# A mean over features made by two float32r products instead of one float32 product

## The chip, the core and the metric

The kernel runs on one core of one Trainium2 chip. A core has a matrix engine (TensorE, PE in the profile), a vector engine (VectorE, DVE), a scalar engine (ScalarE, ACT), a general engine (GpSimd, POOL) and DMA queues, most of them fed here by the sync engine (SyncE, SP). The metric is the device time of one execution in microseconds. The kernel before takes 1026.13 us in the median of three runs (1026.02 to 1029.73).

## The reference, cut to what matters

Three layers follow each other on inputs of 4 batches, 768 positions and 512 features: a chunked attention with 8 heads, a Fourier mixer with a dense block, and a gated convolution block. The change lies in the Fourier mixer, between the transform and the normalization:

```python
X = np.fft.fft(x, axis=1)
X = np.fft.fft(X, axis=2)
u = x + np.real(X)
mu = np.mean(u, axis=-1, keepdims=True)
un = (u - mu) / np.sqrt(np.mean((u - mu) ** 2, axis=-1, keepdims=True) + 1e-06)
ch = np.maximum(un @ w_ch1, 0.0) @ w_ch2
x = u + ch
```

## The kernel before, in words

The program is one long hand-written order. A string of letters (`SCHED`) names the next piece of work for the first two parts: S, E, A, P and X are attention steps of one block of 96 positions (scores, exponentials, transposes, product with the values, transposes of the result), W is a step of decoding a weight, F is a filler product on PE (`keep`), B is the next step of the Fourier transform of a batch (`dft`, a generator that gives up the turn at each `yield`) and D is the next step of the first part of the dense block (`dense`). Each engine executes what it is given in the order in which the program was written, so a letter that adds an instruction to an engine puts it ahead of everything that later letters give to that engine. The first two parts last to about 335 us; the rest of the dense block and the convolution block follow.

Features lie on the 128 partitions, positions along the free dimension. `dft(b)` folds the input (`F`, split in a high float32r part and the rest, `Fh` and `Fl` in the tile `Fhl`), multiplies it with a table (`zstep`, PSUM tile `z`, split again to `zh` by ACT and `zl` by DVE), multiplies that with a second table (PSUM tile `p`) and adds to the spectrum, tiles `G` and `H`, one of even and one of odd parts. The mean over the 512 features needs `G` alone: the two feature blocks of `G` are added (`summed`, tile `gs`, on POOL, one half of 384 positions at a time), and a product with a matrix of constants (`onesm`) sums over the partitions and writes the sum to all partitions (`center`, PSUM tile `pm`). DVE then takes `pm` off `G`, ACT copies one row of `pm` back to the first row of `gs`, and SP writes this row to DRAM (`mud`), from where a later stage reads the mean.

The order around it, for each batch: `summed(0)`, two `zstep`s (c = 2), `center(0)`, `summed(1)`, two `zstep`s (c = 3), `center(1)`. So `summed(1)` is written directly behind `center(0)`, and since `gs` is one buffer, POOL's sum of the second half waits until the row of the first half has been written to DRAM. There are 4 batches and 8 such products.

The names in the rows: `sm` are the attention scores, `atp` and `xtp` PSUM tiles of transposes, `at` and `xT` their copies, `o` the product with the values, `h`, `hh`, `hl`, `y` the tiles of the dense block, `wsc`, `wlb`, `whb` the steps of decoding a weight. `atp`, `xtp`, `idle`, `z`, `p`, `pm`, `h` and `y` take turns in four PSUM buffers (`ps_g`, `PSG = 4`); a new one waits until the copies out of the old one are done. All products of the helper `accumulate` show line 65, the product of `center` line 415.

Of the kernel before, what the change touches and what calls it, by code (L numbers as in the profile page):

```python
# [7 lines left out]
F32 = mybir.dt.float32  # L8
F32R = mybir.dt.float32r
AF = mybir.ActivationFunctionType  # L10
ALU = mybir.AluOpType
# [15 lines left out]
HALF = S // 2  # L27
# [18 lines left out]
def fourier_mixer_kernel(ctx: ExitStack, tc: tile.TileContext, qk, vw, w1, w2, w_in, w_out, conv_w,  # L46
                         mask, ident, dtab, orow, stab, sgn, out):
    nc = tc.nc
    mm = nc.tensor.matmul
# [12 lines left out]
    def accumulate(o, seq, start=True, stop=True):  # L62
        n = len(seq)
        for i, (a, b) in enumerate(seq):
            mm(o, a, b, start=(start and i == 0), stop=(stop and i == n - 1))  # L65

    const = ctx.enter_context(tc.tile_pool(name="const", bufs=1))
    epsc = const.tile([128, 1], F32, name="epsc")
    nc.vector.memset(epsc, 1e-6)
    onesm = const.tile([128, 128], F32, name="onesm")  # L70
    nc.vector.memset(onesm, 2.0 / DM)
    expb = const.tile([128, 1], F32, name="expb")
    nc.vector.memset(expb, -float(EXP0 << 23))
    expl = const.tile([128, 1], F32, name="expl")
# [227 lines left out]
    def dft(b):  # L302
# [10 lines left out]
        Fhl = dfp.tile([128, 20, 193], F32R, tag="Fhl", name="Fhl")  # L313
# [13 lines left out]
        def zstep(c, m):  # L327
            w = SIZES[c]
            w0 = (w + 1) // 2
            s0, sn = (0, w0) if m == 0 else (w0, w - w0)  # L330
            cols = slice(0, CW) if c < 2 else slice(CW, CW + SW)
            nw = CW if c < 2 else SW
            z = ps_g.tile([128, 512], F32, tag="g", name="z")
            terms = []
            for kt in range(2):
                f = FOFF[c] + kt
                terms.append((Fh[:, f, s0:s0 + sn], Fl[:, f, s0:s0 + sn],
                              dtab_sb[:, 0, kt, cols], dtab_sb[:, 1, kt, cols]))
            seq = split3(terms)
            if c < 2:  # L340
                f = FOFF[c] + 2
                seq += [(Fh[0:1, f, s0:s0 + sn], orow_sb), (Fl[0:1, f, s0:s0 + sn], orow_sb)]
            accumulate(z[:sn, 0:nw], seq)
            zh = dfp.tile([97, 256], F32R, tag=f"zh{c % 2}{m}", name="zh")
            zl = dfp.tile([97, 256], F32R, tag=f"zl{c % 2}{m}", name="zl")
            nc.scalar.copy(zh[:sn], z[:sn, 0:256])
            if c < 2:
                zn = dfp.tile([97, 2, 2], F32R, tag=f"zn{c}{m}", name="zn")
                nc.scalar.copy(zn[:sn, 0], z[:sn, 256:258])
            nc.vector.tensor_tensor(out=zl[:sn], in0=z[:sn, 0:256], in1=zh[:sn].bitcast(F32), op=ALU.subtract)  # L350
            if c < 2:
                nc.vector.tensor_tensor(out=zn[:sn, 1], in0=z[:sn, 256:258], in1=zn[:sn, 0].bitcast(F32),
                                        op=ALU.subtract)
                ZN[c, m] = zn
            Z[c, m] = (zh, zl, sn)
# [34 lines left out]
        for m in range(2):  # L390
            zc = slice(128 * m, 128 * m + 128)
            p = ps_g.tile([128, 512], F32, tag="g", name="p")
# [4 lines left out]
                                    in0=pj[:, 0:192, :],  # L397
                                    in1=xT[:, m, 0:384].rearrange("p (j r) -> p j r", r=2), op=ALU.add)
            nc.vector.tensor_tensor(out=G[:, m, 384:385], in0=p[:, 192:193], in1=xT[:, m, 384:385], op=ALU.add)
            nc.vector.tensor_tensor(out=G[:, m, 385:769].rearrange("p (j r) -> p j r", r=2),  # L400
                                    in0=pj[:, 191::-1, ::-1],
                                    in1=xT[:, m, 385:769].rearrange("p (j r) -> p j r", r=2), op=ALU.add)
# [3 lines left out]
        def summed(hf):  # L406
            gs = dfp.tile([128, HALF], F32, tag="gs", name="gs")
            ss = slice(hf * HALF, hf * HALF + HALF)
            nc.gpsimd.tensor_tensor(out=gs, in0=G[:, 0, ss], in1=G[:, 1, ss], op=ALU.add)
            return gs  # L410

        def center(hf, gs):
            ss = slice(hf * HALF, hf * HALF + HALF)
            pm = ps_g.tile([128, 512], F32, tag="g", name="pm")
            mm(pm[:, 0:HALF], onesm, gs, start=True, stop=True)
            for m in range(2):
                nc.vector.tensor_tensor(out=G[:, m, ss], in0=G[:, m, ss], in1=pm[:, 0:HALF], op=ALU.subtract)
            nc.scalar.copy(gs[0:1, :], pm[0:1, 0:HALF])
            nc.sync.dma_start(out=mud[b][:, ss], in_=gs[0:1, :])

        gs = summed(0)
        for c in (2, 3):
            for m in range(2):
                zstep(c, m)
                yield
            center(c - 2, gs)
            if c == 2:
                gs = summed(1)
            yield
        for m in range(2):  # L430
            zc = slice(128 * m, 128 * m + 128)
            p = ps_g.tile([128, 512], F32, tag="g", name="p")
            for c, o, n in ((2, 0, 194), (3, 256, 192)):
                seq = part(c, n, zc)
                accumulate(p[:, o:o + n], seq[:-1], stop=False)
                if m == 0:
# [4 lines left out]
                                    in1=pj[:, 0:192, :],  # L441
                                    in0=xT[:, 2 + m, 0:384].rearrange("p (j r) -> p j r", r=2), op=ALU.subtract)
# [99 lines left out]
    def task(k):  # L542
# [5 lines left out]
        if k == "S":  # L548
            scores(n)
            load_qk(n + 2)  # L550
            if n == 0:
                load_v(2)
        elif k == "E":
            expo(n // 2, n % 2)
            if n == 8:
                nc.gpsimd.dma_start(out=dtab_sb, in_=dtab)
                nc.gpsimd.dma_start(out=orow_sb, in_=orow)
                nc.gpsimd.dma_start(out=stab_sb, in_=stab)
        elif k == "A":
            atr(n // 2, n % 2)  # L560
        elif k == "P":
            pv(n)
            load_v(n + 3)
        elif k == "X":
            xtr(n)
            if n % NU == NU - 2:
                bga.append(dft(n // NU))
        elif k == "F":
            keep(1)
        elif k == "B":  # L570
            return step_of(bga)
        elif k == "D":
            return step_of(bgb)
        else:
            return run(todo[k])
        return True

    with tc.manual_schedule():
# [43 lines left out]
        ps_g.release()  # L622
        ps_g = tc.alloc_tile_pool(name="ps_g2", bufs=3, space=PSUM, reuse_waits="tile")
        uc1 = tc.alloc_tile_pool(name="uc1", bufs=1, reuse_waits="tile")
        onesr = uc1.tile([128, 128], F32R, name="onesr")
        nc.vector.tensor_copy(onesr, onesm)
        NC1 = NB * S // TC

        FS = (range(NI, NI + NGA), range(NI + NGA, NF1), range(NI, NF1))
# [110 lines left out]
        for i, (s, f) in enumerate(seq):  # L740
            c, fs, last = steps[s]
# [283 lines left out]
```

## Time and profile before

| | |
|---|---|
| median of three runs | 1026.13 us (1026.02 to 1029.73) |
| span of the profiled execution, first to last instruction | 1023.3 us |
| PE busy | 1006.2 us, 98% |
| DVE busy | 681.6 us, 67% |
| ACT busy | 442.7 us, 43% |
| POOL busy | 216.8 us, 21% |
| granted clock of PE, mean | 1.000 |
| products `pm` | 8, in 16 records, from 94.2 to 301.6 us |

The span is that of one profiled execution, 2.8 us under the median of the timed runs, which hold the start and the end of the execution too. PE's busy time counts pipelined products whose ends are modelled, so that starts of successive products are the better measure of what one costs.

### The profile page before, as it was taken

How to read it: one execution, taken by the hardware profiler on the slowest of the kernel's cores; microseconds unless marked ns; L12 is line 12 of the kernel's file. 1: busy time of each engine (PE TensorE's matmuls, PEld its weight loads, DVE VectorE, ACT ScalarE, POOL GpSimd, SP SyncE). 2: the span in 40 equal slices, each digit the busy share in tenths (PEclk: the TensorE clock that was granted, in tenths of full speed). 3: DMA queues.
4: the chain of work that ended last, by engine and by line, in shares of the span. 5: the costliest groups of instructions: out<-in, count | busy, mean ns of one | idle time of the engine just before them, and what ended most of it. 6: DMA issues, size and time to landing. Idle time of an engine off the chain costs nothing.

```text
span 1023.3 us, 16696 instructions
## 1 busy us (share of the span) xinstructions
PE 1006.2 (98%) x6446; PEld 959.4 (94%) x6446; DVE 681.6 (67%) x1500; ACT 442.7 (43%) x923; POOL 216.8 (21%) x230
## 2 busy tenths in 40 slices
PE   7899999999999999999999999999999999999998
PEld 6888989999999999999999999999999999999996
DVE  4889956756888766767787775635358566465554
ACT  4687754665433433233333232312245454454442
POOL 1363251432500000112210100202013222222222
PEclk9999999999999999999999999999999999999999
DMA  6864532522236554675879872727543211010101
GB/s 201 265 191 135 170 109 74 159 76 80 104 104 211 185 172 165 204 172 129 196 199 219 200 188 89 112 85 131 180 115 113 70 62 62 1 62 1 62 1 62
DMA packets 63776, 130.87 MB, mean 128 GB/s; under 512 B 4887, under 2 KB 39167, under 8 KB 63471
## 3 DMA queue, kind: packets, MB, share of 16 engines
q1 hardware_dynamic: 51424, 102.35, 30.4%
q0 software_dynamic: 12016, 27.16, 14.7%
q8 instruction: 51, 0.84, 0.3%
q10 hardware_dynamic: 256, 0.28, 0.1%
q14 instruction: 29, 0.24, 0.1%
HBM read 92.28 MB, written 43.79 MB: 133 GB/s over the span
## 4 chain that ended last, share of the span: by engine, by line
PE 90%; DVE 5%; issue 2%; DMA 1%; ACT 1%; POOL 0%; DVEq 0%; ACTq 0%; POOLq 0%
PE acc L65 32%; PE h L65 24%; PE ph L65 12%; PE y L65 5%; PE o L266 4%; PE sc L232 3%; PE z L65 3%; PE p L65 2%; PE atp L255 2%; PE idle L206 1%; PE xtp L291 1%; DVE sm L238 1%; DMA yd<-y 1%; DVE uc L165 1%; DVE wlb L128 0%
## 5 line engine op out<-in xcount | busy, mean ns | idle before, releaser
L65 PE MATMUL acc<-hh,w 128*128 128x384 f32 x768 | 208.0, 334 | 0.0
L65 PE MATMUL h<-uh,w 128*128 128x384 f32 x768 | 208.0, 334 | 0.0
L485 ACT ACTIVATE hh<-h 128x384 fp32r<-128x384 f32 x128 | 62.4, 490 | 247.4 <-PE h L65 247.4
L486 DVE SCALAR_TENSOR_TENSOR hl<-h,hh 128x384 fp32r<-128x384 f32 x128 | 70.6, 555 | 148.2 <-ACT hh L485 147.9
L65 PEld LDWEIGHTS acc<-hh,w 128*128 128x128 f32 x768 | 139.8, 188 | 0.0
L65 PEld LDWEIGHTS h<-uh,w 128*128 128x128 f32 x768 | 139.8, 188 | 0.0
L65 PE MATMUL ph<-xh,wit 128*128 128x384 f32 x512 | 136.3, 337 | 0.7 <-ACT hrow L815 0.7
L65 PE MATMUL acc<-hl,w 128*128 128x384 f32 x384 | 128.3, 334 | 0.0
L65 PE MATMUL h<-ul,w 128*128 128x384 f32 x384 | 128.3, 334 | 0.0
L65 PE MATMUL acc<-wot,hgh 128*128 128x512 f32 x384 | 119.6, 393 | 0.0
L823 DVE SCALAR_TENSOR_TENSOR cv<-hrow,cw_sb,cv 128x768 f32<-128x768 f32 x64 | 110.1, 1721 | 3.1 <-ACT cv L817 2.0
L835 POOL TENSOR_TENSOR hgl<-cv,hgh 128x768 fp32r<-128x768 f32 x32 | 60.3, 1885 | 194.7 <-ACT hgh L834 179.0
L829 DVE TENSOR_TENSOR cv<-hrow,cv 128x768 f32<-128x768 f32 x32 | 30.7, 959 | 99.1 <-ACT cv L828 99.1
L65 PEld LDWEIGHTS ph<-xh,wit 128*128 128x128 f32 x512 | 93.3, 188 | 2.6 <-ACT hrow L815 1.4
L65 PE MATMUL ph<-xl,wit 128*128 128x384 f32 x256 | 86.1, 336 | 0.0
L65 PEld LDWEIGHTS acc<-wot,hgh 128*128 128x128 f32 x384 | 71.7, 188 | 13.4
L246 ACT ACTIVATE sm<-sm,ngm 96x128 f32<-96x128 f32 x256 | 80.5, 392 | 7.3 <-DVE ngm L238 7.3
L815 ACT ACTIVATE hrow<-ph 128x384 f32<-128x384 f32 x64 | 31.2, 493 | 102.3 <-PE ph L65 101.1
L65 PE MATMUL acc<-wot,hgl 128*128 128x512 f32 x192 | 74.7, 389 | 0.0
L65 PEld LDWEIGHTS acc<-hl,w 128*128 128x128 f32 x384 | 72.1, 188 | 0.0
L65 PEld LDWEIGHTS h<-ul,w 128*128 128x128 f32 x384 | 72.1, 188 | 0.0
L238 DVE CUSTOM_DVE_ANT_0 sm<-sc,mask_sb 96x128 f32<-96x128 f32 x256 | 56.3, 281 | 18.6 <-PE sc L232 14.6
(148 smaller groups left out, 1881.3 us busy)
## 6 DMA issues: line engine op xcount, KB each, us to landing
w<-in_w SPq DMA_DIRECT2D x32, 512.0 KB, 4.1
qk<-in_qk SPq DMA_DIRECT2D x32, 448.0 KB, 3.4
us<-ucd SPq DMA_DIRECT2D x13, 768.0 KB, 6.8
yp<-yd SPq DMA_DIRECT2D x13, 768.0 KB, 7.9
vw<-in_vw SPq DMA_DIRECT2D x32, 260.0 KB, 2.9
ucd<-uc SPq DMA_DIRECT2D x8, 768.0 KB, 4.5
yd<-y SPq DMA_DIRECT2D x32, 192.0 KB, 1.9
ucd<-mud POOLq DMA_DIRECT2D x8, 768.0 KB, 14.5
```

The source lines that it names most:

```text
L65: mm(o, a, b, start=(start and i == 0), stop=(stop and i == n - 1))
L232: mm(sch[2 * a + g], qT[64 * g:64 * g + 64, a, :], kT[64 * g:64 * g + 64, a, :], start=True, stop=True)
L238: nc.vector.tensor_tensor_reduce(out=sm[:, h, :], in0=sch[h], in1=mask_sb[:, kind, :], op0=ALU.add, op1=ALU.min, scale=-0.125, scalar=3e38 ...
L246: nc.scalar.activation(out=d["ex"][:, h, :], in_=d["ex"][:, h, :], func=AF.Exp, scale=-1.0, bias=d["ngm"][:, h:h + 1])
L255: nc.tensor.transpose(at[:, i, :], d["ex"][:, 4 * half + i, :], ident_sb[:QB, :QB])
L266: mm(oh[:, h // 4, h % 4, :], at_sb[:, h, :], vw[:, h * (HD + 1):(h + 1) * (HD + 1)], start=True, stop=True)
L485: nc.scalar.activation(out=hh, in_=p[:, 0:TC], func=AF.Relu)
L486: nc.vector.scalar_tensor_tensor(out=hl, in0=p[:, 0:TC], scalar=0.0, in1=hh.bitcast(F32), op0=ALU.max, op1=ALU.subtract)
L815: nc.scalar.activation(out=h[:, 1 + hf * TC:1 + hf * TC + TC], in_=p[:, 0:TC], func=AF.Relu)
L823: nc.vector.scalar_tensor_tensor(out=cv, in0=h[:, j:j + S], scalar=cw_sb[:, j, f:f + 1], in1=cv, op0=ALU.mult, op1=ALU.add)
L829: nc.vector.tensor_tensor(out=cv, in0=h[:, 1:S + 1], in1=cv, op=ALU.mult)
L835: nc.gpsimd.tensor_tensor(out=hgl[i], in0=cv, in1=hgh[i].bitcast(F32), op=ALU.subtract)
```

## The change

The constants get a float32r copy (`onesr`) that is now made at the start of the program, no longer in a later part. `summed` splits its sum: ACT copies `gs` to a float32r tile `gh`, DVE subtracts it from `gs` and writes the rest to `gl`. Both lie in parts of the tile `Fhl` that are no longer needed. `center` multiplies `gh` and `gl` with `onesr`, in two float32r products that add up in `pm`.

```diff
     nc.vector.memset(onesm, 2.0 / DM)
+    onesr = const.tile([128, 128], F32R, name="onesr")
+    nc.vector.tensor_copy(onesr, onesm)
...
             nc.gpsimd.tensor_tensor(out=gs, in0=G[:, 0, ss], in1=G[:, 1, ss], op=ALU.add)
-            return gs
-
-        def center(hf, gs):
+            gh, gl = (Fhl[:, k:k + 2].rearrange("p n w -> p (n w)")[:, 0:HALF] for k in (0, 3))
+            nc.scalar.copy(gh, gs)
+            nc.vector.tensor_tensor(out=gl, in0=gs, in1=gh.bitcast(F32), op=ALU.subtract)
+            return gs, gh, gl
+
+        def center(hf, gs, gh, gl):
             ss = slice(hf * HALF, hf * HALF + HALF)
             pm = ps_g.tile([128, 512], F32, tag="g", name="pm")
-            mm(pm[:, 0:HALF], onesm, gs, start=True, stop=True)
+            accumulate(pm[:, 0:HALF], [(onesr, gh), (onesr, gl)])
...
-            center(c - 2, gs)
+            center(c - 2, *gs)
...
-        onesr = uc1.tile([128, 128], F32R, name="onesr")
-        nc.vector.tensor_copy(onesr, onesm)
```

The order on ACT in the first batch, before; `gs<-pm` is the row of the mean, `zh` the split of the products `z`:

```order
L162 COPY at<-atp 128x384
L346 CAST zh<-z 96x256
L127 ACTIVATE wsc<-wsc,expl 128x512
L346 CAST zh<-z 96x256
L418 COPY gs<-pm 1x384
L346 CAST zh<-z 97x256
L346 CAST zh<-z 96x256
L296 ACTIVATE xT<-xtp 128x4x96
```

The same place on ACT now; `Fhl<-gs` is the new copy `gh`:

```order
L164 COPY at<-atp 128x384
L413 CAST Fhl<-gs 128x384
L348 CAST zh<-z 96x256
L129 ACTIVATE wsc<-wsc,expl 128x512
L348 CAST zh<-z 96x256
L423 COPY gs<-pm 1x384
L413 CAST Fhl<-gs 128x384
L348 CAST zh<-z 97x256
L348 CAST zh<-z 96x256
L298 ACTIVATE xT<-xtp 128x4x96
```

The first copy stands ahead of both `zh` of c = 2, the second directly behind the row of the mean and ahead of both `zh` of c = 3.

The order on ACT in the third batch, around the row of the first half, before:

```order
L162 COPY y<-y 128x384
L346 CAST zh<-z 96x256 x2
L162 COPY at<-atp 128x384
L418 COPY gs<-pm 1x384
L162 COPY at<-atp 128x384
L346 CAST zh<-z 97x256
```

The same place on ACT now:

```order
L164 COPY y<-y 128x384
L413 CAST Fhl<-gs 128x384
L348 CAST zh<-z 96x256 x2
L164 COPY at<-atp 128x384
L423 COPY gs<-pm 1x384
L413 CAST Fhl<-gs 128x384
L164 COPY at<-atp 128x384
L348 CAST zh<-z 97x256
```

Here the second copy stands ahead of a copy `at` out of a PSUM buffer.

The order on DVE in the fourth batch, at the second half of the mean, before:

```order
L417 TENSOR_TENSOR G<-G,pm 128x384 x2
L135 TENSOR_SCALAR wsc<-whb 128x512
L139 SCALAR_TENSOR_TENSOR w_5_3822<-wlb,wsc 128x512
L123 TENSOR_SCALAR wsc<-w_4113 128x512
L124 TENSOR_SCALAR wlb<-w_4113 128x512
L128 SCALAR_TENSOR_TENSOR wlb<-w_4113,wlb 128x512
L350 TENSOR_TENSOR zl<-z,zh 97x256
```

The same place on DVE now; `Fhl<-gs,Fhl` is the new subtraction `gl`:

```order
L422 TENSOR_TENSOR G<-G,pm 128x384 x2
L414 TENSOR_TENSOR Fhl<-gs,Fhl 128x384
L137 TENSOR_SCALAR wsc<-whb 128x512
L141 SCALAR_TENSOR_TENSOR w_5_3842<-wlb,wsc 128x512
L125 TENSOR_SCALAR wsc<-w_4133 128x512
L126 TENSOR_SCALAR wlb<-w_4133 128x512
L130 SCALAR_TENSOR_TENSOR wlb<-w_4133,wlb 128x512
L352 TENSOR_TENSOR zl<-z,zh 97x256
```

The subtraction stands behind the one that takes the mean off `G`, and ahead of five steps of decoding and the next `zl`.

## Rows read from the trace of the kernel before

**Rows 1.** The page: the span, and busy time, share and instructions of each engine

```profile
span 1023.3 us, 16696 instructions
PE 1006.2 (98%) x6446; PEld 959.4 (94%) x6446; DVE 681.6 (67%) x1500; ACT 442.7 (43%) x923; POOL 216.8 (21%) x230
```

**Rows 2.** Busy us by stretch: length, PE, PEld, DVE, ACT, POOL, clock, DMA share, GB/s

```profile
0.00:85.00 85.00, 76.02 (x757) 67.20 (x758) 62.91 (x342) 58.60 (x171) 30.54 (x54) 1.00 0.69 212
85.00:110.00 25.00, 24.83 (x250) 22.79 (x249) 22.53 (x93) 16.84 (x51) 6.67 (x12) 1.00 0.43 129
```

**Rows 3.** Waits of PE up to 335 us: the longest (total, times, longest)

```profile
PE sc L232 <- DMA qk<-in_qk: 2.2, 1, 2.2
```

**Rows 4.** Instructions on gs and pm: ns min/median/max, first and last start, form

```profile
L409 POOL TENSOR_TENSOR gs<-G x8: 864/866/871, 93.2 to 297.3; 128x384 f32<-128x384 f32 x8
L418 ACT COPY gs<-pm x8: 467/469/471, 96.7 to 305.5; 1x384 f32<-1x384 f32 x8
L417 DVE TENSOR_TENSOR G<-G,pm x16: 539/545/554, 95.6 to 304.9; 128x384 f32<-128x384 f32 x16
```

**Rows 5.** Timeline of PE, second batch: start, duration, instruction [idle before it, and releaser]

```profile
166.06 0.84 PE L415 MATMUL pm<-gs,onesm 128*128 128x384 f32 x2
...
166.91 0.33 PE L65 MATMUL h<-ul,rxa 128*128 128x384 f32 x1
167.07 0.34 PE L65 MATMUL h<-uh,rxb 128*128 128x384 f32 x1
```

**Rows 6.** Timeline of the first batch, several engines

```profile
93.24 0.87 POOL L409 TENSOR_TENSOR gs<-G 128x384 f32<-128x384 f32 x1 [1.85 <-DVE G L396]
...
93.71 0.42 DVE L350 TENSOR_TENSOR zl<-z,zh 96x256 fp32r<-96x256 f32 x1
...
95.58 1.01 DVE L417 TENSOR_TENSOR G<-G,pm 128x384 f32<-128x384 f32 x2
...
96.68 0.47 ACT L418 COPY gs<-pm 1x384 f32<-1x384 f32 x1 [2.12 <-DVE G L417]
97.06 0.62 ACT L346 CAST zh<-z 97x256 fp32r<-97x256 f32 x2
97.17 0.31 SPq L419 DMA_DIRECT2D mud<-gs  x1
...
98.42 0.86 POOL L409 TENSOR_TENSOR gs<-G 128x384 f32<-128x384 f32 x1 [4.32 <-ACT sm L246]
...
101.89 0.46 ACT L162 COPY at<-atp 128x384 f32<-128x384 f32 x1
...
103.10 0.45 PE L65 MATMUL p<-stab_sb,zh 96*128 96x194 f32 x2
```

**Rows 7.** Timeline of the second batch, ACT and PE

```profile
169.03 0.49 ACT L485 ACTIVATE hh<-h 128x384 fp32r<-128x384 f32 x1 [0.53 <-PE h L65]
...
172.81 0.33 PE L65 MATMUL y<-hh,rxc 128*128 128x384 f32 x1
```

**Rows 8.** Timeline of the third batch, ACT, SP and PE

```profile
233.95 0.46 ACT L162 COPY at<-atp 128x384 f32<-128x384 f32 x1
...
234.07 0.24 SPq L419 DMA_DIRECT2D mud<-gs  x1
...
234.47 0.44 PE L65 MATMUL y<-hh,rxc 128*128 128x384 f32 x1
```

**Rows 9.** Timeline of the fourth batch, DVE, SP and PE

```profile
295.39 0.42 DVE L135 TENSOR_SCALAR wsc<-whb 128x512 int32<-128x512 int32 x1
...
296.05 0.24 SPq L419 DMA_DIRECT2D mud<-gs  x1
...
297.36 1.34 DVE L128 SCALAR_TENSOR_TENSOR wlb<-w,wlb 128x512 int32<-128x512 int32 x1
298.62 0.41 DVE L350 TENSOR_TENSOR zl<-z,zh 97x256 fp32r<-97x256 f32 x1
...
299.09 0.45 PE L65 MATMUL h<-uh,rxa 128*128 128x384 f32 x1
```

## The prediction

> **What bounds the kernel now.** First the busy times of the page: PE is busy 1006 of 1023 us, so some 17 us of idle time are left in all [rows 1]. Then the busy times by stretch: 9 of these 17 us lie in the first 85 us; where the change works, PE has 0.2 us of idle time in 25 us, and DVE is nearly as full, 22.5 of 25 us [rows 2]. So the end is set by PE's list: what shortens it is gained, and what makes PE wait is lost, for hardly any idle time is left behind it to give the loss back. Then the timelines around the eight means. PE, ACT and DVE each take their lists in order, so the question for every added instruction is what it waits for and what stands behind it.
>
> **What is saved.** The float32 product starts at 166.06; the second `h` product behind it starts at 166.91, and such products follow each other by 0.16 us, so the first `h` began at about 166.74 and the mean cost 0.68 us [rows 5]. Two float32r products of the same 384 columns cost 2 x 0.16 to 0.17, or 0.33. Saved: 0.35 us at each of 8 places, 2.8 us, all on PE.
>
> **What is added.** Eight copies on ACT and eight subtractions on DVE. The nearest rows are ACT's copy of 384 columns, 0.47 us, and DVE's subtraction of as many, 0.55 us [rows 4]. If they merely filled idle time they would cost nothing; DVE has too little of it for that in the first batch, and the waits are worse than the work. The copy waits for POOL's sum `gs`, the subtraction for the copy, and both stand ahead of what PE wants next. The copy `onesr` moves from the later part to the start, where DVE has nothing else to do: nothing.
>
> The second half of each mean is the bad one. Its `gs` waits until the first half's row is in DRAM. In the first batch: ACT starts that row at 96.68, SP issues the transfer at 97.17, 0.49 later, and POOL starts at 98.42, 1.25 after the issue [rows 6]; POOL needs 0.87 [rows 4]. Until now nobody but PE waited for that, much later. Now ACT stops behind the row's copy until 0.49 + 1.25 + 0.87 = 2.6 us after its start, which is some 2.2 us of standing still, then copies 0.47, and DVE, which had finished with `G` before the row was copied, stands still for 3.1 us before its 0.55. Everything that the two have behind that comes later. What PE feels of it differs from batch to batch.
>
> First batch. POOL's first sum ends at 94.11 (93.24 + 0.87), the copy at about 94.64, the subtraction at about 95.2. DVE used to start `zl` at 93.71 and `G` minus `pm` at 95.58 [rows 6]; it now starts that list at 95.2, 1.5 us later, and the row of the mean starts at 98.1. By the sum above, POOL's second sum starts at 99.85 and ends at 100.72, and the copy ends at 101.25. ACT's `zh`, formerly at 97.06, starts at about 101.2, a shift of 4.1 us. From there ACT is busy almost without a break to the copy `at` at 101.89 (to 102.35), and the second half of PE's products `o` waits for this copy: eight heads, then `p` at 103.10 [rows 6]. So `p` comes at 107.1 at the earliest, 4.0 late, both savings already inside. DVE, full on both sides of the place, can't get it back.
>
> Second batch. Long `h` products stand around both halves. The first copy falls behind `hh` in a gap of ACT and delays nothing. At the second half ACT's `hh`, at 169.03, comes at about 170.8 and its rest on DVE at about 172.0, but PE needs them only in the last three products of `y`, from 172.81, or 172.4 with the saving [rows 7]. No wait: 2 x 0.35 = 0.7 us gained.
>
> Third batch. At the first half DVE is about 0.5 us late, so the row's transfer, at 234.07 before, is issued at 234.56. POOL starts at 235.80 and ends at 236.67, the copy ends at 237.2, and only then ACT copies `at`, formerly at 233.95, to 237.57. `y`, formerly at 234.47, needs the PSUM buffer that this frees: it starts at 237.6, 3.15 late [rows 8]. Less 0.35 for the second product: 2.8 lost.
>
> Fourth batch. At the first half the subtraction ends at about 293.0, and its product, 0.17 after the other, just finds it; DVE is 0.35 late. The transfer goes from 296.05 to 296.4, POOL ends at 298.5, the copy at 299.0, the subtraction at 299.6. Then come the five steps of decoding that DVE did from 295.39 on, 3.2 us until `zl` at 298.62, where PE's `h` already waited for the buffer that `zl` frees, at 299.09 [rows 9]. The last of the five, 1.34 long from 297.36 on, ran beside POOL's sum, twice as long as I take it to be alone; now POOL is done by then, so the five take 2.6: `zl` from 302.2 to 302.6, `h` at 302.7, 3.6 late. Less 0.35: 3.25 lost.
>
> **Sum.** +4.0 - 0.7 + 2.8 + 3.25 = +9.35 us. On the profiled execution, 1023.3 + 9.35 = 1032.6; the median of the runs lies 2.8 above that span, hence 1035.5 us. From both sides: if PE felt nothing, -2.8; if every batch lost as much as the first, +16.
>
> **The rivals.** Not slower: the stops of ACT and DVE stay hidden. PE then keeps 2.8 us, 1023.3 us, which is within 0.5% of before (5.1 us, about what can be told from no change here). The place where it decides is the second half: PE must have some 3.5 us of products in front of it that need nothing new from ACT or DVE. The second batch shows such a place [rows 7]; in the third and fourth PE starts less than 0.1 us after ACT's copy (233.95 + 0.46) or DVE's `zl` (298.62 + 0.41) used to free its buffer [rows 8, 9], which speaks against it.
>
> Half is given back: engines that had been late find slack later, about 5 us lost, 1031. The idle time in front of the place, 9 of 17 us, is past by then [rows 2], so this is thin.
>
> PE's clock falls in a gap. In this trace it was granted at 1.00, the upper of its two levels, through gaps of up to 2.2 us [rows 2, 3]; the gap of the fourth batch is 3.6 us. At half the clock twelve products of 0.16 to 0.17 would take about 4 us for 2; one or two such groups make 2 to 4 us, so 1037.5 to 1039.5. The Trainium skill (TensorE: Matmul & The Clock Gate, "Why this matters for your kernels") warns of idle gaps between bursts of products, after which the clock goes back to half; by that rule a gap as long as the fourth batch's would bring this case, while the shorter gaps of this trace did not.
>
> The change doesn't do what it says: the two float32r products take as long as the one float32 product. Then 2.8 us are not saved and the time is 1038.3. Against it stands the spacing of 0.16 us of the `h` products, of the same type and width [rows 5].
>
> **How the numbers follow.** Forecast 0.62, time 1035.5, its own range 1032.5 to 1039. Hidden 0.12, half given back 0.05, clock 0.14, no cheaper products 0.07. Slower by over 0.5%, above 1031.3, takes the forecast, the clock and the dear products: 0.83. Within 0.5%: the half and nearly all of the hidden case, 0.15; faster 0.02. The range of 8 in 10, 1029 to 1041, leaves out the hidden case and the far end of the clock.
>
> **What would show it.** In the changed profile: ACT idle some 2.2 us before each second copy, released by POOL, and DVE some 3 us before each second subtraction; PE waits of 2 to 4 us on ACT or DVE in the first, third and fourth batch and none in the second; a spacing of 0.16 us between the two products of a mean; a clock of 1.00 at about 303. The forecast is wrong if these stops are there and PE shows no new waits behind them, or if the waits are there and the span grows by less than half of them.

## The result, and the profile after

The changed kernel takes 1038.62 us (median of 4 runs, 1038.16 to 1038.84), beside 1027.93 us of the kernel before on the same chip (4 runs, 1026.02 to 1029.73): a ratio of 1.0115, 95% interval 1.0091 to 1.0139. It is slower, as forecast, 3.1 us above the 1035.5 us forecast and inside the range. In some executions of most kernels here the granted clock falls already in the first 85 us and the run is some 4 us longer, and the medians hold these too (two of the four runs of the kernel before took 1029.73 us, the others 1026.0 and 1026.1; of the experiments below, five of the twelve runs of the products without the split and six of the twelve of the later product with the split on POOL, whose other six took 1026.1 to 1027.0), so stages are compared from 85.88 us on.

The page of the profile after, first lines, against [rows 1]:

```profile
span 1036.8 us, 16713 instructions
PE 1009.6 (97%) x6446; PEld 963.7 (93%) x6446; DVE 686.0 (66%) x1508; ACT 445.7 (43%) x931; POOL 216.1 (21%) x230
```

The span grew by 13.5 us. ACT and DVE have 8 instructions more each, and only 3.0 and 4.4 us more busy time. Even if all of these 7.4 us had been in PE's way, the work itself would be little over half of the loss.

The waits of PE after, us in total, times, longest, from 60 to 345 us; before, the longest of the program was 2.2 us and lay in the first 85 us [rows 3]:

```profile
PE h L65 <- DVE zl L352: 3.9, 1, 3.9
PE y L65 <- ACT at L164: 2.5, 1, 2.5
PE idle L208 <- DVE zl L352: 1.8, 1, 1.8
...
PE o L268 <- ACT at L164: 0.9, 1, 0.9
PE xtp L293 <- ACT gs L423: 0.8, 1, 0.8
PE pm L65 <- ACT Fhl L413: 0.7, 1, 0.7
```

The first is the forecast gap of the fourth batch (`h` waits for `zl`), the second that of the third (`y` waits for the copy `at`). The 1.8, 0.9 and 0.7 us lie in the first batch, the 0.8 us of `xtp` in the third, and none in the second.

What stands behind them, the instructions on `gs` (ns min/median/max, first and last start, form) and what ended the idle time of their engines before them (us, times), against [rows 4]:

```profile
L411 POOL TENSOR_TENSOR gs<-G x8: 862/866/870, 93.3 to 305.9; 128x384 f32<-128x384 f32 x8
L413 ACT CAST Fhl<-gs x8: 506/511/513, 94.2 to 306.8; 128x384 fp32r<-128x384 f32 x8
L414 DVE TENSOR_TENSOR Fhl<-gs,Fhl x8: 548/558/559, 94.8 to 307.3; 128x384 fp32r<-128x384 f32 x8
...
DMA mud<-gs: 19.9, 4
ACT Fhl L413: 15.5, 6
POOL gs L411: 15.2, 6
```

POOL waits four times for the row on its way to DRAM, ACT for POOL, and DVE for ACT. One link of it, the timeline of the first batch, against [rows 6] (start, duration, instruction, idle before it and releaser):

```profile
98.20 0.47 ACT L423 COPY gs<-pm 1x384 f32<-1x384 f32 x1 [2.32 <-DVE G L422]
...
98.76 0.31 SPq L424 DMA_DIRECT2D mud<-gs  x1
...
100.02 0.86 POOL L411 TENSOR_TENSOR gs<-G 128x384 f32<-128x384 f32 x1 [5.83 <-DMA mud<-gs]
...
100.91 0.51 ACT L413 CAST Fhl<-gs 128x384 fp32r<-128x384 f32 x1 [2.24 <-POOL gs L411]
101.33 0.63 ACT L348 CAST zh<-z 97x256 fp32r<-97x256 f32 x2
...
101.46 0.56 DVE L414 TENSOR_TENSOR Fhl<-gs,Fhl 128x384 fp32r<-128x384 f32 x1 [3.34 <-ACT Fhl L413]
...
107.06 0.45 PE L65 MATMUL p<-stab_sb,zh 96*128 96x194 f32 x2
```

From the issue to POOL's start it is 1.26 us, as long as the 1.25 us of [rows 6], where POOL's wait was still put down to ACT's `sm`; ACT stands still for 2.24 and DVE for 3.34 us, and `zh` comes at 101.33, not at 97.06. `p` starts at 107.06; 107.1 was forecast.

What was not in the forecast's sum is the clock. Stretches of 2 us in the third and the fourth batch, columns as in [rows 2]:

```profile
242.00:244.00 2.00, 2.00 (x8) 2.00 (x7) 0.55 (x2) 0.00 (x0) 0.00 (x0) 0.50 0.00 0
...
308.00:310.00 2.00, 0.00 (x0) 0.00 (x0) 1.90 (x5) 0.58 (x1) 0.00 (x0) 1.00 0.00 0
310.00:312.00 2.00, 1.09 (x3) 1.09 (x4) 2.00 (x5) 1.30 (x4) 0.00 (x0) 0.54 0.00 0
312.00:314.00 2.00, 2.00 (x8) 2.00 (x8) 1.81 (x5) 0.76 (x3) 0.00 (x0) 0.50 0.67 211
```

The granted clock is 0.50, the lower of the two levels, behind both long gaps: PE is full (2.00) and gets through 8 products in 2 us. The products `h` behind the fourth gap, against [rows 9]:

```profile
310.91 0.69 PE L65 MATMUL h<-uh,rxa 128*128 128x384 f32 x1 [3.88 <-DVE zl L352]
311.40 0.52 PE L65 MATMUL h<-ul,rxa 128*128 128x384 f32 x1
311.72 0.52 PE L65 MATMUL h<-uh,rxb 128*128 128x384 f32 x1
```

They follow each other by 0.32 us; such products before stood 0.16 apart in [rows 5], and 0.17 to 0.19 further down the same chain.

Where the 13.5 us arise is read by subtracting, product by product, the starts on PE in the two profiles (us late against before, at the first product of its kind behind the place):

| late by, us | at entry | `p`, 1st batch | `xtp`, 2nd | `xtp`, 3rd | `y`, 4th | `y`, later |
|---|---|---|---|---|---|---|
| start before | 85.88 | 103.10 | 183.16 | 245.17 | 305.68 | 323.36 |
| after | 0.08 | 3.96 | 3.49 | 7.89 | 14.28 | 13.27 |

So the batches cost +3.88, -0.47, +4.40 and +6.39 us, and 1.01 us come back later. Each kernel's figures are read from one profiled execution.

### The profile page after: what moved, and what is told of

Same layout as the page of the kernel before. It is cut to its first block, busy times and chain, and to the rows that moved or that the text cites. A ratio compares the mean times of both kernels' runs of the same rounds, so it can differ in the third digit from the quotient of the medians.

```text
span 1036.8 us, 16713 instructions
## 1 busy us (share of the span) xinstructions
PE 1009.6 (97%) x6446; PEld 963.7 (93%) x6446; DVE 686.0 (66%) x1508; ACT 445.7 (43%) x931; POOL 216.1 (21%) x230
## 4 chain that ended last, share of the span: by engine, by line
PE 90%; DVE 5%; issue 2%; ACT 1%; DMA 1%; POOL 1%; POOLq 0%; ACTq 0%; DVEq 0%; SPq 0%
PE acc L65 32%; PE h L65 25%; PE ph L65 12%; PE y L65 6%; PE o L268 3%; PE sc L234 3%; PE p L65 3%; PE z L65 2%; PE atp L257 2%; PE idle L208 1%; DVE sm L240 1%; PE xtp L293 1%; POOL gs L411 0%; DVE wlb L130 0%; DMA qk<-in_qk 0%
```

## The experiments

They ran on four chips, each beside the kernel before, whose median there is 1025.3 to 1025.6 us; a ratio is to that. What each stage cost stands in a table at the end of this section.

**The row in a place of its own.** The changed kernel, with the row of the mean in `row`, an unused end of `G`'s tile:

```diff
-            nc.scalar.copy(gs[0:1, :], pm[0:1, 0:HALF])
-            nc.sync.dma_start(out=mud[b][:, ss], in_=gs[0:1, :])
+            nc.scalar.copy(row, pm[0:1, 0:HALF])
+            nc.sync.dma_start(out=mud[b][:, ss], in_=row)
```

> The row of the mean is copied to a place of its own (the unused end of the tile of G) and no longer onto gs, so that POOL's second sum does not wait for the write to DRAM; all else as in the changed kernel. Theory (ACT and DVE stand still behind that write, and PE waits for them and then runs some products at half the clock): the stops of 2.2 us on ACT and 3.3 us on DVE go, PE's waits of 2.5 us (y, third batch) and 3.9 us (h, fourth) go, the clock stays at 1.00; what is left is the 1.5 us by which the first split delays DVE in the first batch, less 8 savings of 0.24 us: 1027.5 us, between 1026 and 1030. Rival (the price is the added work itself, eight copies of 0.51 us on ACT and eight subtractions of 0.56 us on DVE): the time stays above 1034 us, with waits of PE on ACT or DVE at the same places.

Measured: 1031.23 us, ratio 1.006 (1.0042 to 1.0078). Of the 13.2 us that the stages of the changed kernel lose, 6.1 are left (table at the end of this section). The time lies between the theory's 1030 and the rival's 1034: the write to DRAM, with the clock's falls behind it, cost more than half, but another wait took the place of the one removed. Timeline of this run in the third batch:

```profile
234.68 0.72 POOL L279 TENSOR_TENSOR xf<-xn 96x256 f32<-96x256 f32 x1
235.37 0.86 POOL L413 TENSOR_TENSOR gs<-G 128x384 f32<-128x384 f32 x1
...
236.26 0.51 ACT L415 CAST Fhl<-gs 128x384 fp32r<-128x384 f32 x1 [1.24 <-POOL gs L413]
...
237.20 0.45 PE L65 MATMUL y<-hh,rxc 128*128 128x384 f32 x1 [1.51 <-ACT at L164]
...
237.70 0.52 PE L65 MATMUL y<-hh,rxd 128*128 128x384 f32 x1
238.02 0.52 PE L65 MATMUL y<-hh,rxc 128*128 128x384 f32 x1
```

POOL does its sums of `xf` first, in program order, and the clock falls again behind a gap of 0.71 and one of 1.51 us (products 0.32 apart).

**The split without its products.**

```diff
-            accumulate(pm[:, 0:HALF], [(onesr, gh), (onesr, gl)])
+            mm(pm[:, 0:HALF], onesm, gs, start=True, stop=True)
```

> The split into gh and gl is made, but the mean is still one float32 product of gs. Theory (stops of ACT and DVE): all waits as in the changed kernel, and the product dearer by 0.24 us at places where PE does not wait behind it: 1038.6 + 0.5 to 1.9 us, so 1039 to 1040.5 us. Rival (the two products are what costs, through their waits for gh and gl): pm needs only gs and starts early again, 1028 to 1033 us.

Measured: 1040.64 us, ratio 1.0151 (1.013 to 1.0171). Just above the theory's end, far from the rival's: PE has no longer anything to do with `gh` and `gl`, and the waits of 3.6 (`h`) and 2.5 us (`y`) stand. The split costs all, the products save.

**The products without the split.** The low part is left out, and the row has its own place as above.

```diff
-            gs = dfp.tile([128, HALF], F32, tag="gs", name="gs")
+            gs = dfp.tile([128, HALF], F32R, tag="gs", name="gs")
...
-            nc.scalar.copy(gh, gs)
-            nc.vector.tensor_tensor(out=gl, in0=gs, in1=gh.bitcast(F32), op=ALU.subtract)
-            return gs, gh, gl
+            return gs, gs, gs
```

> The two float32r products without the split: POOL writes its sum rounded to float32r and both products read it (the low part is left out, so the mean is doubled and rounded); the row of the mean has a place of its own. Theory: only the saving is left, 8 x 0.24 us = 1.9 us, up to 2.8 us if the pair takes 0.33 us: 1025 to 1026 us beside 1027.9 us of before. Rival (the products are no cheaper in their place): 1027.5 to 1028.5 us.

Measured: 1024.53 us, ratio 1.0001 (0.9988 to 1.0014), no difference that the times show. The trace shows one: the products behind a mean come 0.29 us earlier at each place where PE waits for nothing, 1.9 us in all from 85.88 to 323.36 us.

**The second split later,** behind the first product `z` of c = 3:

```diff
                 zstep(c, m)
+                if c == 3 and m == 0:
+                    gs = split(gs)
                 yield
```

> The second split of each mean is written behind the first product group z of c = 3 (behind its copy zh and its rest zl), not directly behind the first product of the mean; the wait for the write to DRAM stays. Theory (the engines stand still in program order): the copies that freed PSUM buffers now run ahead of the stop, so PE's waits in the first, third and fourth batch shrink, the time lies at 1033 us (1029 to 1036). Rival (work itself, or the wait wherever it stands): 1037 to 1040 us.

Measured: 1033.26 us, ratio 1.0086 (1.0066 to 1.0107), as the theory had it, but not by its steps. In the third and fourth batch the loss is gone (0.09 and 0.43 us), in the first it is not (3.60), and 3.8 us are new, behind the fourth. Timeline of ACT, SP and PE there:

```profile
315.51 0.24 SPq L427 DMA_DIRECT2D mud<-gs  x1
...
318.73 0.52 SPq L468 DMA_DIRECT2D ucd<-uc  x1
319.30 1.67 SPq L513 DMA_DIRECT2D yd<-y  x2
...
324.93 0.95 ACT L164 COPY y<-y 128x384 f32<-128x384 f32 x2 [4.41 <-DMA yd<-y]
...
325.46 0.44 PE L65 MATMUL h<-uh,rxa 128*128 128x384 f32 x1 [2.94 <-ACT y L164]
```

SP issues the writes `yd` behind `ucd`, in its own order; ACT's copy `y` waits for such a write, and `h` for the copy. Before, the same wait of `h` was 0.72 us; in the changed kernel it is not there, which is most of the 1.01 us that came back. Why the write comes later here than before wasn't followed further.

**Both sums early.** POOL adds both halves before anything else; the splits stay.

```diff
-        gs = summed(0)
+        gs, g1s = split(*summed(0)), summed(1)
...
-                gs = summed(1)
+                gs = split(*g1s)
```

> POOL adds both halves one behind the other as soon as G is there (the second into the unused end of the tile of G, with its row), so that neither the write to DRAM nor POOL's later work on xf stands ahead of the second sum; the splits stay where the changed kernel has them. In the kernel where the row alone had a place of its own, ACT still waited 1.24 us for the second sum in the third batch, because it stood behind xf in POOL's list, and the clock fell there. Theory: that wait and that fall go (about 2.5 us), the 1.5 us of the first batch and some 1.6 us in the fourth (DVE waits for row copy and gh, 1.0, then 0.56 for gl) stay: 1028.5 us, 1027 to 1030, where before takes 1025.3. Rival (the added work is the rest of the price): 1030.5 to 1031.5 as in that kernel.

Measured: 1028.36 us, ratio 1.0029 (1.0018 to 1.004), the theory. The clock is 1.00 again; what is left in the fourth batch is `h` waiting for `zl`:

```profile
PE h L65 <- DVE zl L352: 1.3, 1, 1.3
```

**Both sums early, both splits later.**

```diff
                 zstep(c, m)
+                if m == 0:
+                    gs = split(*sums[c - 2])
                 yield
```

> Both sums early as in the kernel beside it, and each split written behind the first zstep of its c (so ACT has zh and DVE zl ahead of it). Theory (only order costs): the eight savings of 0.29 us are left, less about 1 us in the first batch, where pm comes as soon as gs is there and now waits for gh and gl: 1024.3 us, 1023 to 1026, where before takes 1025.3. Rival (added work of 0.51 and 0.56 us costs wherever it stands): 1028 us or more.

Measured: 1027.38 us, ratio 1.0017 (1.0006 to 1.0028): between theory and rival, over the range. The second, third and fourth batch now cost nothing (-0.11, -0.08, -0.01), but gain at most a tenth of a microsecond and not 0.58 each: in the second and fourth `pm` waits 0.15 to 0.17 us at a time for the split, and in the third `xtp` waits 0.54 us for the row's copy. The first batch loses 1.31.

**The split on POOL,** sums early:

```diff
-            nc.scalar.copy(gh, gs)
-            nc.vector.tensor_tensor(out=gl, in0=gs, in1=gh.bitcast(F32), op=ALU.subtract)
+            nc.gpsimd.tensor_copy(gh, gs)
+            nc.gpsimd.tensor_tensor(out=gl, in0=gs, in1=gh.bitcast(F32), op=ALU.subtract)
```

> Both sums early, and copy and subtraction on POOL, nothing added to ACT and DVE. Theory: no stop of ACT or DVE is left, but the first pm comes 2 x 0.87 us later than gs, which PE feels where pm followed gs at once (94.11 and 94.16 us in the first batch) and not where products stand in between: 1.7 us in one to three batches, less 8 x 0.29: 1025.5 us, 1023.5 to 1028.5, where before takes 1025.3. Rival (the two products themselves bring the loss): 1029 us or more.

Measured: 1027.08 us, ratio 1.0014 (1.0005 to 1.0024), inside the theory's range. Nothing is added to ACT and DVE, and the batches cost +2.20, -0.58, -0.27 and -0.59 us. The longest wait for the split, and what POOL did in the first batch:

```profile
PE pm L65 <- POOL Fhl L418: 1.8, 1, 1.8
```

```profile
94.10 0.87 POOL L412 TENSOR_TENSOR gs<-G 128x384 f32<-128x384 f32 x1 [1.84 <-DVE G L399]
95.03 1.53 POOL L418 CAST Fhl<-gs 128x384 fp32r<-128x384 f32 x1
96.64 0.99 POOL L419 TENSOR_TENSOR Fhl<-gs,Fhl 128x384 fp32r<-128x384 f32 x1
```

There the product needs `gs` as soon as it is made, so every step between the two is felt.

**Gaps filled.** The changed kernel with 18 products repeated ahead of each of its two long gaps:

```diff
+            if (b, c, m) == (2, 3, 1):
+                for _ in range(3):
+                    accumulate(z[:sn, 0:nw], seq)
             accumulate(z[:sn, 0:nw], seq)
...
+        if (c, f) == (5, 2):
+            accumulate(p[:, 0:TC], seq + seq[:6])
         accumulate(p[:, 0:TC], seq)
```

> The changed kernel with products repeated ahead of its two longest gaps of PE: the six products z ahead of xtp and y in the third batch are run four times (18 more), the twelve products h ahead of the gap in the fourth two and a half times (18 more); the results are the same. The gap of 2.5 us becomes about 1, that of 3.9 to 4.2 us about 1. Theory (the slow stretches of 3 to 5 us behind these gaps are the clock's fall in the gap): the granted clock stays 1.00 at 240 to 250 and at 310 to 318 us, about 1.6 and 2.6 us come back: 12.5 - 4.2, so 8 to 10 us above before, 1034.5 us. Rival (the products behind the gaps are slow for another reason, or the added products delay what follows): the time stays 12 us or more above before.

Measured: 1035.01 us, ratio 1.0089 (1.0076 to 1.0102), the theory. The same stretches as after (the third batch, the fourth):

```profile
242.00:244.00 2.00, 1.91 (x11) 1.91 (x12) 1.47 (x4) 0.58 (x3) 0.00 (x0) 1.00 0.03 8
...
312.00:314.00 2.00, 2.00 (x18) 1.97 (x17) 1.97 (x5) 1.33 (x3) 0.00 (x0) 1.00 0.66 246
```

With 36 products more the kernel is faster than the changed one, 9.0 us of loss in the stages beside 13.2. In these two places the clock stays up, behind gaps of 1.3 and 0.8 us; the third batch costs 2.84 us and not 4.40, the fourth 3.62 and not 6.39. So the clock's share is 1.6 and 2.8 us, and the waits' share 2.84 and 3.62. In the first batch of this same run, where nothing was changed, the clock fell behind the gap of 1.8 us ahead of `idle` (0.50 from 104 to 106 us), as it did in the run with the split alone behind 1.9 us; in the changed kernel it stayed at 1.00 behind the same 1.8 us. It cost almost nothing there (+3.96 against +3.88): PE's slow products ran through the 0.9 us in which `o` waits for `at` otherwise.

**The first product of the mean later,** behind the first `z` of c = 3, with the split on POOL; with the float32 product of before; and with the copies on ACT, the subtractions on DVE:

```diff
-        for c in (2, 3):
-            for m in range(2):
-                zstep(c, m)
-                yield
-            center(c - 2, *sums[c - 2])
-            yield
+        for step in ((2, 0), (2, 1), (3, 0), 0, (3, 1), 1):
+            if step in (0, 1):
+                center(step, *sums[step])
+            else:
+                zstep(*step)
+            yield
```

> As the kernel with copy and subtraction on POOL, and the first product of the mean changes places with the next product group z (c = 3, first half). Theory: what that kernel lost to before lay in the first batch alone (pm waited 1.8 and 0.6 us for POOL); with the z products in between the wait shrinks by 0.7 to 1.4 us (six z products), and the savings of 0.29 us stay: 1025 us, 1023.5 to 1026.5, where before takes 1025.6. Rival (a later pm makes G and the row late, and something else waits): 1027 us or more.

> The kernel before, its float32 product kept, with the same exchange of the first product of the mean and the next z. Control for the run beside it: theory, the exchange alone is worth nothing, as pm never waited: 1025.6 us, 1024.5 to 1027. Rival: the exchange itself gains or costs over 1.5 us, and the run beside it shows that and not the split.

> Both sums early on POOL, copies on ACT and subtractions on DVE both written behind the second z of c = 2, and the first product of the mean behind the first z of c = 3. Theory (only order costs): PE's wait in the first batch (about 1.3 us net) goes, the savings of 0.29 us stay in all places: 1024 us, 1023 to 1026, where before takes 1025.6. Rival (0.51 us on ACT and 0.56 us on DVE eight times are in the way wherever they stand): 1027 us or more.

Measured: 1027.93 us, ratio 1.002 (1.0007 to 1.0034), with POOL, in the rival's range by the median, though its stages add up to 0.7 us only; 1024.03 us, ratio 0.9979 (0.9967 to 0.999), with the product of before; 1025.96 us, ratio 1.0001 (0.999 to 1.0011), with ACT and DVE, 2 us over the theory's time, at the end of its range. The first batch stays dear: +1.49 with POOL and +2.08 with ACT and DVE, where the exchange alone is at -0.26. The control was needed, and its theory was wrong: the exchange is worth 1.5 us by itself and not nothing, of which 1.02 arises behind the fourth batch, where `h` waited for `y`. The trace shows most of what the first batch still loses, with POOL:

```profile
96.73 0.44 PE L65 MATMUL pm<-Fhl,onesr 128*128 128x384 f32 x1 [1.05 <-POOL Fhl L418]
97.81 0.44 PE L65 MATMUL pm<-Fhl,onesr 128*128 128x384 f32 x1 [0.64 <-POOL Fhl L419]
```

The first product still waits for the copy, 1.05 us and not 1.76, and the second for the subtraction as long as without the exchange. With ACT and DVE the two waits are 0.32 and 0.72 us; `o` waits another 0.26 us for `at`, and the rest of the 2.08 us wasn't followed up.

**Each where it pays.** The exchange everywhere; float32 product in the first and fourth batch, split on POOL in the second and third:

```diff
+            if b in (0, 3):
+                return gs, gs, None
...
+            if gl is None:
+                mm(pm[:, 0:HALF], onesm, gs, start=True, stop=True)
+            else:
+                accumulate(pm[:, 0:HALF], [(onesr, gh), (onesr, gl)])
```

> The first product of the mean behind the next z in all batches; in the first and fourth batch the float32 product as before, in the second and third the two float32r products with copy and subtraction on POOL. Theory (the product pair saves 0.29 us wherever nobody waits for the split): the kernel before with that exchange alone takes 1.5 us less than before, and four savings of 0.29 us come on top: 2.7 us under before, 1022.9 us (1022.2 to 1023.8) where before takes 1025.6. Rival (the split costs somewhere else what the products save): 1023.7 to 1025 us, as with the exchange alone.

Measured: 1023.05 us beside 1025.33 of before, ratio 0.9977 (0.9965 to 0.999): the theory, and faster than the kernel before and the changed one. The times don't tell it from the exchange alone (0.9979, 0.9967 to 0.999, on another chip); that the four pairs add 1.2 us to the exchange stands in the stages alone, -2.7 us in all against -1.55.

What each stage cost or gained against before, us, by the same subtraction of starts:

| kernel | 1st batch | 2nd | 3rd | 4th | later |
|---|---|---|---|---|---|
| changed | +3.88 | -0.47 | +4.40 | +6.39 | -1.01 |
| row of its own | +1.46 | -0.53 | +3.36 | +1.63 | +0.22 |
| split alone | +4.34 | +0.10 | +4.76 | +6.32 | -1.00 |
| products alone | -0.29 | -0.58 | -0.32 | -0.84 | +0.13 |
| second split later | +3.60 | -0.51 | +0.09 | +0.43 | +3.81 |
| both sums early | +1.64 | -0.50 | +0.68 | +1.00 | +0.24 |
| both splits later | +1.31 | -0.11 | -0.08 | -0.01 | +0.25 |
| split on POOL | +2.20 | -0.58 | -0.27 | -0.59 | +0.21 |
| gaps filled | +3.96 | -0.40 | +2.84 | +3.62 | -1.01 |
| exchange alone | -0.26 | +0.02 | -0.22 | -0.07 | -1.02 |
| exchange, split on POOL | +1.49 | -0.58 | -0.82 | +0.38 | +0.21 |
| exchange, split on ACT, DVE | +2.08 | -0.59 | -0.81 | +0.55 | -1.02 |
| each where it pays | -0.26 | -0.56 | -0.80 | -0.09 | -1.01 |

## Why the prediction was right, and where it fell short

- **The time alone** doesn't decide. 1038.62 us lies in the forecast's own range (1032.5 to 1039), but also where the clock's rival (1037.5 to 1039.5) and the rival of products no cheaper (1038.3) put it. The traces decide: the forecast waits are there, the products are cheaper, and the clock fell on top.
- **The saving.** Forecast 0.35 us at each place; the runs show 0.29, so the rival of products no cheaper is out. Behind long products, in the third batch, before and after:

```profile
240.14 0.81 PE L415 MATMUL pm<-gs,onesm 128*128 128x384 f32 x2
...
240.98 0.27 PE L65 MATMUL p<-stab_sb,zl 96*128 96x194 f32 x1
```

```profile
248.32 0.51 PE L65 MATMUL pm<-Fhl,onesr 128*128 128x384 f32 x2
248.67 0.36 PE L65 MATMUL p<-stab_sb,zh 96*128 96x194 f32 x2
248.87 0.28 PE L65 MATMUL p<-stab_sb,zl 96*128 96x194 f32 x1
```

From the mean to the same product `p` it is 0.84 us before and 0.55 after. The pair takes 0.35 us here, where 0.33 was forecast, and so the float32 product 0.64 and not 0.68.

- **First batch,** +4.0 forecast, +3.88 measured, by the steps given: 2.24 us on ACT, 3.34 on DVE, `p` at 107.06. The last wait is the forecast one (`o` for `at`, 0.9 us); 1.8 us of waiting came earlier, at a filler product `idle` that waits for `zl`, which the forecast doesn't name. The run with the row in its own place shows that the second half's stop is 2.4 us of it; 1.46 belong to the first half, where `gs` is needed at once.
- **Second batch,** -0.7 forecast, -0.47 measured: no wait, only the smaller saving. ACT stood still there too, 2.21 us, ahead of `hh`, and nobody felt it [rows 7]:

```profile
174.40 0.51 ACT L413 CAST Fhl<-gs 128x384 fp32r<-128x384 f32 x1 [2.21 <-POOL gs L411]
174.82 0.48 ACT L490 ACTIVATE hh<-h 128x384 fp32r<-128x384 f32 x1
```

- **Third batch,** +2.8 forecast. The wait is as forecast ([rows 8]: `y` from 234.47, 3.51 late at entry, to 241.08; 3.1 late by the stop), and the batch without the clock's fall costs 2.84. The forecast has no word on the 0.8 us that `xtp` waits ahead of it for the row's copy. The clock adds 1.6.
- **Fourth batch,** +3.25 forecast; 3.62 without the clock, since the transfer took 1.54 us from issue to POOL and not 1.25, and the five steps of decoding on DVE 2.65 as taken [rows 9]. The clock adds 2.8.
- **Later,** nothing forecast; 1.01 us come back, where `h` waited for a copy `y` before.
- **The step that failed** is the clock. It was a rival at 0.14 and 2 to 4 us, "one or two such groups", and the forecast itself expected 1.00 behind the fourth batch's gap; it came in both gaps, on top of the forecast's waits, and is worth 1.6 + 2.8 = 4.4 us. It was priced a little low and held too unlikely: the prediction asks only about the gap of the fourth batch, and not about that of the third. The rule of the Trainium skill (TensorE: Matmul & The Clock Gate, "Why this matters for your kernels") that gaps between bursts bring the clock to half holds for the fourth batch's 3.88 us. The traces go further than the page, and where the two differ the traces decide: shorter gaps did it too (2.94 us in the run with the second split later; 2.5 us in the third batch, close behind one of 0.8; 1.51 us close behind one of 0.71 in the run with the row in its own place), gaps of 1.3 and 0.8 us, with products added ahead of them, did not, and one of 1.8 us in the first batch did in the run with the gaps filled and not in the changed kernel. So the length of a gap alone doesn't decide it here.
- **The sum.** 1023.3 + 9.35 + 4.4 - 1.0 = 1036.0, beside a span of 1036.8; the smaller savings and the longer transfer make up most of the rest. The span was thus missed by 4.2 us (1032.6 forecast), and that the median is only 3.1 us off is luck in part: each timed run lies 1.8 us above its own span, and the forecast took 2.8, which compared a span with the times of other executions. The 1.0 us that came back behind the fourth batch was luck as well.

## What to carry to other kernels

An added copy or subtraction is priced by what it waits for and by what stands behind it on its engine, not by its duration: here two copies and two subtractions of 0.5 us cost PE 2.8 to 3.9 us in three of the four batches, without the clock's share, in large part because a single buffer tied them to a write to DRAM that only PE, much later, had waited for. Look for the chain through every engine that works in order, POOL's and SP's lists too; when the first wait was removed, the next item on POOL's list took its place. And where PE is full on both sides, price a gap twice, once for the wait and once for the products that may follow it at half the clock: here behind gaps of 2.5, 2.9 and 3.9 us, and once it cost nothing, where PE had another wait to come.

## What the runs showed of the hardware

- Products added into two gaps made the kernel faster: 36 more products, 4.2 us less between 85.88 and 323.36 us, the granted clock 1.00 behind them where it had been 0.50.
- Behind a gap of 2.94 us in the run with the second split later the clock fell as well, after three products:

```profile
325.74 0.37 PE L65 MATMUL h<-ul,rxa 128*128 128x384 f32 x1
325.92 0.52 PE L65 MATMUL h<-uh,rxb 128*128 128x384 f32 x1
326.24 0.52 PE L65 MATMUL h<-uh,rxa 128*128 128x384 f32 x1
```

- A step of decoding on DVE that took 1.34 us before, beside POOL's sum [rows 9], took 0.69 us in the changed kernel, where POOL's sum was over by then, as the forecast had taken it:

```profile
309.75 0.69 DVE L130 SCALAR_TENSOR_TENSOR wlb<-w,wlb 128x512 int32<-128x512 int32 x1
```

- With the split on POOL, its copy of 128x384 with a change of type took 1.53 us for the first half of the first batch, 0.51 us for the second half, and 0.50 to 0.51 us in five of the other six (0.85 in one):

```profile
98.53 0.51 POOL L418 CAST Fhl<-G 128x384 fp32r<-128x384 f32 x1
```
